# A four-layer attention/Fourier kernel: weight rows spread over more buffers, sequence products moved among TensorE's instructions

## The chip, the cores and the metric

One core of a Trainium2 chip runs the whole program in one launch. The metric is the device time of one execution in microseconds (us). Each kernel is run several times and the median is compared. The profile is one further execution on the same core, recorded by the hardware profiler. Engines are called PE (TensorE), PEld (its weight loads), DVE (VectorE), ACT (ScalarE), POOL (GpSimd) and SP (SyncE, which here issues nearly all DMAs).

## The reference

The input x has 2048 rows of 640 numbers in f32. Four layers follow one another, each added to its input:

```
x = x + A(layernorm(x));  x = x + B(layernorm(x));  x = x + A(layernorm(x));  x = x + B(layernorm(x))

A: qkv = x @ wqkv                     # 32 heads of 20
   row s looks at rows s, s-2, ..., s-14   # 8 keys, dilation 2, masked below 0
   o = softmax(q.k * 20**-0.5) . v
   return o @ wo
B: a = x @ dft_hid_re.T;  b = x @ dft_hid_im.T
   return dft_seq_re @ a - dft_seq_im @ b   # 2048 x 2048 sequence matrices
```

The matrices of B are inputs like any other: the kernel may not use that they hold sines and cosines.

## The kernel before

Every f32 matrix product is made of three fp32r products: each operand is split into a rounded high part (a cast, on ACT) and the remaining low part (a subtraction, on DVE or POOL), and high x high, high x low and low x high are added up in PSUM (`PASSES`). `split(hi, lo, src)` does this (L130 the cast, L132 and L134 the subtraction).

**Attention layers (`layer_a`, run for layers 0 and 2).** The 2048 rows are 4 chunks c of 4 tiles j of 128 rows. The loop is a plan written out by hand: `at(step, phase, fn, ...)` puts a piece of work into a step (about -8 to 66) and a phase, and the loop over steps and `PHASES` issues the pieces in that order on all engines (`manual_schedule(engines=ENGINES)`). Within a step the phases run `peT0 dma evac hi pe peL pe2 ... actL ... misc dmac dmar pe3w pe3`. One step holds half a unit of attention: the products q*k on DVE (L435) with a halving on POOL (L438) and a reduction on DVE (L445), the softmax on small tiles (L453 the exponential on ACT, L462 to L470 on DVE), the products with v on DVE (L475), and their sums on POOL (L494 to L496; the very last on DVE, L491). TensorE meanwhile makes qkv (`qkv_mm`, L366), transposes the attention output (`pc_pe`, L331; `pc_hi` casts it on ACT, L335; `pc_sub` subtracts the high part in PSUM with the negative identity, L339; `pc_lo` copies out the low part, L354, or on DVE, L352) and multiplies it by wo (`wo_mm`, L519). `wo_add` (L163, DVE) adds the residual out of PSUM and sums up for the layernorm; `wo_stats` (ACT L168, L170, L174), `wo_fin` (POOL L178), `ln_hi` or `ln_tail` (ACT L908, L924; DVE L925) and `ln_lo` (L912) make the split, normalized rows of the next layer.

**Sequence products in the attention layers.** The first of the eight output tiles of the following layer B is begun inside the attention layer. `z_mm(s, p)` (L979) adds the products of sequence tile s (16 of them) to five PSUM banks; p is a third of them, 5 matmuls of 128 x 512, and None is all 15. `ZTHIRDS[ly]` says how many thirds stand at which step; thirds at step 52 go into phase `pe2`, the others into `pe3`. The split sequence tile comes from DRAM (`c_get`, L957) or is loaded and split in place (`c_load` L934, `c_hi` L938, `c_lo` L966). Buffers s0, s2 and s3 take turns. After the last step the remaining pieces are issued in a written order: the transposes `pc_pe(67)`, `wo_mm` for tiles 2 and 3 of the last chunk, and `z_mm` for tiles 13, 14 and 15 with the layernorm tails between them.

**Spectral layers (`LayerB`).** `run` copies the first output tile out of PSUM (`evac`, `zt_put`, L1034 to L1041), calls `load_w`, and then goes on with the next tile's sequence products (`zpart`), of which only TensorE's order is written out. The order on the other engines, and the place of their DMAs on SP, is made by a scheduler when the program is built, also against the end of the attention layer. `load_w` loads the five row blocks of the two hidden matrices, real and imaginary in turn, ten loads of 320 KB through the two buffers of tag xa, and splits each (the imaginary ones negated) into r2a (real, after wo is done with it) and pr0 to pr3 and zo3 (imaginary; pr0 to pr3 are the product buffers of the attention layer). `ymm` (L1061) uses them. Meanwhile `x_whole` and `x_combine` (L1106 to L1120) make sums of row blocks and store them to DRAM through tags stg and xa for a Strassen-like scheme (`pair`, `product` L1158), which covers the other output tiles.

The tag stg has two buffers, used by `qkv_evac`, by `c_load`, and later by `x_combine`.

Of the kernel before, what the change touches and what calls it, by code (L numbers as in the profile page):

```python
# [11 lines left out]
F32R = mybir.dt.float32r  # L12
# [8 lines left out]
D = 640  # L21
# [5 lines left out]
P = 128  # L27
# [3 lines left out]
KD = D // P  # L31
# [15 lines left out]
WSTEP = (0, 0, 0, 1, 1, 2, 2, 3, 3, 4, 4, 5, 5, 6, 7)  # L47
WHOLE = ((43, 45, 47, 49, 51, 55, 57, 59, 63), (51, 57, 63))
ZTHIRDS = (
    {49: 3, 50: 3, 51: 2, 52: 1, 53: 2, 54: 1, 56: 3, 57: 6, 58: 3, 59: 4, 60: 2, 61: 1, 62: 3, 63: 4, 64: 1},  # L50
    {50: 3, 51: 5, 52: 1, 53: 1, 54: 1, 55: 1, 56: 5, 57: 4, 58: 3, 59: 3, 60: 1, 61: 1, 62: 4, 63: 2, 64: 4},
)
TA = 65
# [25 lines left out]
def tile_layers(ctx: ExitStack, tc: tile.TileContext, x, wqkv, wo, cs, wre, wim, out):  # L79
    nc = tc.nc  # L80
# [9 lines left out]
    def nm(base):  # L90
        uid[0] += 1
        return f"{base}_{uid[0]}"

    def T(shape, tag, dt=F32, bufs=1, pool=None):
        return (pool or sb).tile(shape, dt, tag=tag, name=nm(tag), bufs=bufs)

    def pt(shape, tag, bufs=1):
        return ps.tile(shape, F32, tag=tag, name=nm(tag), bufs=bufs)
# [30 lines left out]
    def split(hi, lo, src, neg=False, eng=None):  # L129
        nc.scalar.activation(hi, src, AF.Copy, scale=-1.0 if neg else 1.0)  # L130
        if neg:
            nc.vector.scalar_tensor_tensor(lo, src, -1.0, hi.bitcast(F32), op0=ALU.mult, op1=ALU.subtract)  # L132
        else:
            (eng or nc.vector).tensor_tensor(lo, src, hi.bitcast(F32), op=ALU.subtract)  # L134
# [62 lines left out]
    def load_x(src, j, tag="xa"):  # L197
        xt = T([P, D], tag, bufs={"xa": 2}.get(tag, 1))
        nc.sync.dma_start(xt, src[:, j, :])
        return xt  # L200
# [45 lines left out]
    def layer_a(li, stats, handoff, prev):  # L246
        xin, xout = xs[li], xs[li + 1]
        first = li == 0
# [19 lines left out]
        def at(step, phase, fn, *args):  # L268
            plan.setdefault((step, phase), []).append((fn, args))
# [41 lines left out]
        def pc_pe(step):  # L311
            banks, out = {}, []
            for kind, c, j, k0, k1, bank, col, tag in pieces[step]:
                if tag and tag.startswith("r1"):
                    if j == 2:
                        oT["pair"] = T([P, 2, 2, KD, P], tag, F32R)
                    oT[(c, j)] = oT["pair"][:, j - 2]
                elif tag:
                    (xnT if kind == "x" else oT)[(c, j, 1) if kind == "x" else (c, j)] = T([P, 2, KD, P], tag, F32R)
                src, st = (  # L320
                    (xnT[(c, j)], xnT[(c, j, 1)]) if kind == "x" else (oo[(c, j // 2)][:, j % 2], oT[(c, j)])
                )
                if bank not in banks:
                    banks[bank] = (pt([P, 512], bank), [])
                pb, todo = banks[bank]
                todo += [(pb[:, col + i * P : col + (i + 1) * P], src[:, k * P : (k + 1) * P]) for i, k in enumerate(range(k0, k1))]
                out.append((pb[:, col : col + (k1 - k0) * P], st, k0, k1))
            pieces[step] = out
            for pb, todo in banks.values():
                for i, (dst, src) in enumerate(todo):  # L330
                    nc.tensor.matmul(dst, src, ident, start=i == 0, stop=i == len(todo) - 1, is_transpose=True)  # L331

        def pc_hi(step):
            for pb, st, k0, k1 in pieces[step]:
                nc.scalar.copy(st[:, 0, k0:k1], pb.rearrange("p (k f) -> p k f", f=P))  # L335
# [12 lines left out]
        def pc_lo(step, vec=False):  # L348
            for pb, st, k0, k1 in pieces[step]:
                pv = pb.rearrange("p (k f) -> p k f", f=P)  # L350
                if vec:
                    nc.vector.tensor_tensor(st[:, 1, k0:k1], pv, st[:, 0, k0:k1].bitcast(F32), op=ALU.subtract)  # L352
                else:
                    nc.scalar.copy(st[:, 1, k0:k1], pv)  # L354
# [155 lines left out]
        def wo_mm(c, j, banks, e0=0, e1=2, k0=0, k1=KD):  # L510
            if e0 == 0 and k0 == 0:
                oT[(c, j, "m")] = []
            for e in range(e0, e1):
                if k0 == 0:
                    oT[(c, j, "m")].append(pt([P, 512], banks[e]))
                m = oT[(c, j, "m")][e]
                for i, (a, b) in enumerate(PASSES):
                    for k in range(k0, k1):
                        nc.tensor.matmul(  # L519
                            m[:, :320],  # L520
                            oT[(c, j)][:, a, k],
                            wo_s["w"][:, b, k, e * 320 : (e + 1) * 320],
                            start=(i, k) == (0, 0),
                            stop=(i, k) == (2, KD - 1),
                        )

        def wo_add(c, j, e0=0, e1=2, store=True):
            for e in range(e0, e1):
                if e == 0 and j == 0:
                    nstats[c] = Stats()  # L530
                nstats[c].add(j, e, xr[(c, j)], oT[(c, j, "m")][e][:, :320])
            if e1 == 2 and store:
                wo_store(c, j)
# [4 lines left out]
        def wo_stats(c, j):  # L538
            nstats[c].added(j, xr[(c, j)])

        def wo_fin(c, j0, j1):
            nstats[c].finish(j0, j1)
# [282 lines left out]
        thirds = [t for t, n in ZTHIRDS[ly].items() for _ in range(n)]  # L825
# [6 lines left out]
        for z in range(len(thirds) // 3):  # L832
            t = thirds[3 * z]
            if first and z in PRE:
                at((46, 47, 49)[z] if z < 3 else max(thirds[3 * z - 7] + 1, t - 3), "dmac", handoff.c_get, z)
            elif first:
                at(t - 2, "dmac", handoff.c_load, z)
                at(t - 1, "hi", handoff.c_hi, z)
                at(t - 1, "misc", handoff.c_lo, z, z in (11, 12))
            else:  # L840
                at(min(t - 1, 48 + z) if z < 3 else t - 1, "dmac", handoff.c_get, z)
            for p in range(3):
                at(thirds[3 * z + p], "pe2" if thirds[3 * z + p] == 52 else "pe3", handoff.z_mm, z, p)
        if first:
            at(62, "dmac", handoff.c_load, 13)
            at(63, "hi", handoff.c_hi, 13)
# [8 lines left out]
        with tc.manual_schedule(engines=ENGINES):  # L855
            if first:
                prologue_first()
            nc.vector.tensor_copy(mk, mask)
            for s in range(LEAD0[0], last + 1):
                for ph in PHASES:  # L860
                    for fn, args in plan.pop((s, ph), ()):
                        fn(*args)
            pc_pe(67)
            pc_hi(67)
            pc_lo(67, True)
            wo_mm(c, 2, None, 0, 2, 3)
            wo_mm(c, 3, ("pq", "aux0"))
            wo_add(c, 2)
            wo_stats(c, 2)
            wo_fin(c, 2, 3)  # L870
            if first:
                handoff.c_hl(14)
            handoff.z_mm(13, None)
            handoff.ln_tail(c, 2, xr, nstats)
            wo_add(c, 3)
            handoff.ln_lo(c, 2)
            handoff.z_mm(14, None)
            wo_stats(c, 3)
            wo_fin(c, 3, 4)
            if first:  # L880
                handoff.c_hl(15)
            handoff.ln_tail(c, 3, xr, nstats)
            handoff.ln_lo(c, 3)
            handoff.z_mm(15, None)
# [4 lines left out]
    class LayerB:  # L889
# [95 lines left out]
                )  # L985

        def load_w(self):
            self.wr = T([P, 2, KD, D], "r2a", F32R)
            self.wi = []
            for k in range(KD):  # L990
                raw = load_x(wre, k)
                split(self.wr[:, 0, k], self.wr[:, 1, k], raw)
                raw = load_x(wim, k)
                if k < 4:
                    wt = T([P, 2, D], f"pr{k}", F32R)
                    hl = (wt[:, 0], wt[:, 1])
                else:
                    wt = T([P, 2, D], "zo3", F32R)
                    hl = (wt[:, 0], wt[:, 1])
                split(hl[0], hl[1], raw, neg=True)  # L1000
                self.wi.append(hl)

        def cw_load(self, t, s):
            self.raw[s] = wtile([P, 512])
# [324 lines left out]
    st0 = [None] * NC  # L1329
    b1, b2 = LayerB(1), LayerB(3)  # L1330
    layer_a(0, st0, b1, None)
    st2 = [None] * NC
    b1.run(st2)
    layer_a(2, st2, b2, b1)
    b2.run(None)
    b2.ytile(NT - 1, 0, None)
# [56 lines left out]
```

## Time and profile before

| | us |
|---|---|
| three runs | 1764.7, 1770.85, 1773.08 |
| median | 1770.85 |
| profiled execution, its own time | 1764.77 |
| its span | 1762.9 |
| PE busy | 1735.4 (98%) |
| DVE busy | 1378.4 (78%) |
| ACT busy | 809.2 (46%) |
| POOL busy | 622.0 (35%) |

The span runs from the first to the last recorded instruction; the execution's own time has some us around it. Matmuls are pipelined, and the busy time of PE counts each until its modelled end, so a busy PE is not one at its peak. In the rows of a timeline stand the start, the duration, the engine, the line of the kernel, the operation, the tiles (output <- inputs) and, in brackets, how long the engine had been idle before and what ended that. "x30" merges 30 instructions of a kind. A line of the waits says who waited for whom: us in total, times, longest. In the span the first attention layer ends near 390 us, the second runs from about 860 to 1262 us.

### The profile page before, as it was taken

What the parts mean: (1) busy time and instruction counts of PE and PEld (TensorE: products, weight loads), DVE (VectorE), ACT (ScalarE), POOL (GpSimd) and SP (SyncE); (2) the same over time, 40 slices, a digit from 0 to 9 for tenths busy, and PEclk for the clock granted to TensorE, in tenths of its full rate; (3) what the DMA queues carried; (4) which work ended last, traced back from release to release, by engine and by line L of the source; (5) the groups of instructions that cost most, each with busy time, mean ns of one, the idle gap of its engine ahead of it and who ended that gap; (6) DMA issues with size and microseconds to landing.
All of it is one profiled execution on the core that took longest, in us unless ns stands there. A gap on an engine that the chain in (4) does not pass through costs nothing.

```text
span 1762.9 us, 26454 instructions
## 1 busy us (share of the span) xinstructions
PE 1735.4 (98%) x8798; PEld 1506.6 (85%) x8798; DVE 1378.4 (78%) x2131; ACT 809.2 (46%) x1682; POOL 622.0 (35%) x585
## 2 busy tenths in 40 slices
PE   9999998989999999999999999999999999999999
PEld 7889897878888888888998889988788888888888
DVE  6999999988767767767648999999777676687673
ACT  4564544554445444445534344444434443443441
POOL 4799998840000000000028998899100000000000
PEclk9999999999999999999999999999999999999999
DMA  8996769748777777686657866798587767767761
GB/s 287 314 317 206 224 205 327 263 166 309 266 254 252 247 252 229 223 272 224 201 182 228 270 209 214 218 332 275 196 311 261 253 212 246 253 217 244 253 202 53
DMA packets 273961, 426.20 MB, mean 242 GB/s; under 512 B 22656, under 2 KB 153728, under 8 KB 273568
## 3 DMA queue, kind: packets, MB, share of 16 engines
q1 hardware_dynamic: 270624, 422.54, 72.2%
q10 hardware_dynamic: 3200, 1.97, 0.4%
q8 instruction: 70, 1.15, 0.3%
q14 instruction: 67, 0.55, 0.1%
HBM read 339.28 MB, written 85.14 MB: 241 GB/s over the span
## 4 chain that ended last, share of the span: by engine, by line
PE 69%; DVE 15%; DMA 7%; POOL 3%; issue 3%; ACT 3%; SPq 0%; DVEq 0%; ACTq 0%; POOLq 0%
PE m L366 14%; PE aux L1061 14%; PE t L1158 11%; PE m L1158 11%; PE pq L1158 5%; PE xt L1158 5%; PE aux L519 4%; DVE pr L435 3%; DVE pr L475 2%; DMA xc<-stg 2%; DVE lg L445 1%; POOL pr L494 1%; PE m L979 1%; PE t L979 1%; DMA xa<-wre_in 1%
## 5 line engine op out<-in xcount | busy, mean ns | idle before, releaser
L366 PE MATMUL m<-r,s 128*128 128x480 f32 x1920 | 436.1, 381 | 0.4 <-DVE r L649 0.2
L366 PEld LDWEIGHTS m<-r,s 128*128 128x128 f32 x1920 | 355.6, 188 | 53.8 <-DVE r L649 1.0
L1061 PE MATMUL aux<-r2a,zo 128*128 128x320 f32 x768 | 226.5, 310 | 0.0
L1151 ACT CAST r<-win 128x512 fp32r<-128x512 f32 x246 | 150.2, 620 | 159.7 <-DVE win L1187 65.4
L494 POOL TENSOR_TENSOR pr<-pr 128x640 f32<-128x640 f32 x126 | 206.3, 1637 | 32.3 <-DVE pr L475 31.5
L1061 PE MATMUL aux<-pr,zo 128*128 128x320 f32 x704 | 208.3, 308 | 0.0
L178 POOL TENSOR_TENSOR stats<-stats,mhalf 128x1 f32<-128x1 f32 (+1 forms) x40 | 29.4, 734 | 497.0 <-ACT stats L174 487.7
L1152 DVE TENSOR_TENSOR r<-win,r 128x512 fp32r<-128x512 f32 x246 | 165.5, 687 | 46.4 <-ACT r L1151 44.4
L435 DVE TENSOR_TENSOR pr<-pq,win 128x1280 f32<-128x1280 f32 x128 | 189.7, 1483 | 8.9 <-ACT pq L408 5.8
L475 DVE TENSOR_TENSOR pr<-pq,win 128x1280 f32<-128x1280 f32 x128 | 190.7, 1491 | 5.0
L438 POOL TENSOR_TENSOR pr<-pr 128x640 f32<-128x640 f32 x116 | 166.8, 1438 | 15.6 <-DVE pr L435 15.2
L1158 PE MATMUL m<-r,r 128*128 128x512 f32 x594 | 152.6, 392 | 0.0
L1061 PEld LDWEIGHTS aux<-r2a,zo 128*128 128x128 f32 x768 | 144.1, 188 | 1.9
L1158 PE MATMUL t<-r,r 128*128 128x512 f32 x498 | 135.7, 394 | 0.0
L1061 PEld LDWEIGHTS aux<-pr,zo 128*128 128x128 f32 x704 | 132.2, 188 | 2.1
L1158 PEld LDWEIGHTS m<-r,r 128*128 128x128 f32 x594 | 111.4, 188 | 24.6
L979 PE MATMUL m<-s,r 128*128 128x512 f32 x384 | 118.6, 396 | 4.9 <-POOL s L966 1.7
L445 DVE TENSOR_REDUCE lg<-pr 128x64 f32<-128x640 f32 (+1 forms) x128 | 112.1, 876 | 8.9 <-POOL pr L438 8.5
L979 PE MATMUL t<-s,r 128*128 128x512 f32 x384 | 118.2, 395 | 0.4 <-DVE ot L1036 0.3
L495 POOL TENSOR_TENSOR pr<-pr 128x320 f32<-128x320 f32 x126 | 112.1, 890 | 9.9
L1158 PEld LDWEIGHTS t<-r,r 128*128 128x128 f32 x498 | 93.9, 188 | 21.6
L373 ACT COPY stg<-m 128x480 f32<-128x480 f32 x128 | 71.0, 555 | 84.9 <-PE m L366 64.3
(295 smaller groups left out, 3216.1 us busy)
## 6 DMA issues: line engine op xcount, KB each, us to landing
win<-cs_in SPq DMA_DIRECT2D x351, 256.0 KB, 3.8
r<-xc SPq DMA_DIRECT2D x240, 256.0 KB, 4.2
win<-kvb SPq DMA_DIRECT2D x96, 440.0 KB, 4.3
xa<-cs_in SPq DMA_DIRECT2D x121, 256.0 KB, 4.1
win<-kvb SPq DMA_DIRECT2D x64, 360.0 KB, 4.9
kvb<-stg SPq DMA_DIRECT2D x60, 320.0 KB, 5.2
xc<-stg SPq DMA_DIRECT2D x32, 512.0 KB, 4.0
s<-c0b SPq DMA_DIRECT2D x26, 512.0 KB, 5.8
```

What stands on the lines that cost most here:

```text
L366: nc.tensor.matmul(mt[g][:, : 3 * F], st[:, a, k], wq[q][:, b, k], start=n == 0, stop=n == 14)
L435: nc.vector.tensor_tensor(pr, q, wview(u, jp, 0, [[1, FE]]), op=ALU.mult)
L438: nc.gpsimd.tensor_tensor(pv[:, :, 0:10], pv[:, :, 0:10], pv[:, :, 10:20], op=ALU.add)
L445: nc.vector.tensor_reduce(lgs[u][:, :, 2 * jp : 2 * jp + 2].rearrange("p h j w -> p (j w) h"), prq.pop((u, jp)), axis=AX.X, op=ALU.add,)
L475: nc.vector.tensor_tensor(pr.rearrange("p j w (h d) -> p j w h d", d=DH), lgs[u][:, :, 2 * jp : 2 * jp + 2].rearrange("p h j w -> p j w h" ...
L494: g.tensor_tensor(pr[:, :, 0:4], pr[:, :, 0:4], pr[:, :, 4:8], op=ALU.add)
L495: g.tensor_tensor(pr[:, :, 0:2], pr[:, :, 0:2], pr[:, :, 2:4], op=ALU.add)
L979: self.last = nc.tensor.matmul(self.z[t][k], self.xn[c][:, a, j, k * P : (k + 1) * P], self.ct[s][:, b], start=s == 0 and i == 0, stop=s = ...
L1061: self.last = nc.tensor.matmul(self.ym[e][:, :320], zt[(k, a, ri)][:, j2 * P : (j2 + 1) * P], w[:, e * 320 : (e + 1) * 320], start=(k, a, ...
L1151: nc.scalar.copy(hi, raw)
L1152: nc.vector.tensor_tensor(lo, raw, hi.bitcast(F32), op=ALU.subtract)
L1158: nc.tensor.matmul(bank, w(a, kb), hl[b], start=start and (a, b) == (0, 0), stop=stop and (a, b) == (1, 0),)
```

## The change

Three things are changed. (1) In the first attention layer four thirds of sequence products stand at step 52, none at 53 and 54 (before: one, two and one), and in this layer those of step 52 go into phase `pe`, ahead of the products of `pc_sub`, where they stood behind them. (2) In the second attention layer two thirds of tile 13 are issued ahead of the last transposes, and the third at the place where all three stood. (3) `load_w` issues its loads into tiles of its own: the first real and the first imaginary row into the two stg buffers, the second ones into the two xa buffers, and the rest through xa; and r2a is taken over only after the first load has been issued.

```diff
 ZTHIRDS = (
-    {49: 3, 50: 3, 51: 2, 52: 1, 53: 2, 54: 1, 56: 3, 57: 6, 58: 3, 59: 4, 60: 2, 61: 1, 62: 3, 63: 4, 64: 1},
+    {49: 3, 50: 3, 51: 2, 52: 4, 56: 3, 57: 6, 58: 3, 59: 4, 60: 2, 61: 1, 62: 3, 63: 4, 64: 1},
...
-                at(thirds[3 * z + p], "pe2" if thirds[3 * z + p] == 52 else "pe3", handoff.z_mm, z, p)
+                at(thirds[3 * z + p], "pe" if first and thirds[3 * z + p] == 52 else "pe2" if thirds[3 * z + p] == 52 else "pe3", handoff.z_mm, z, p)
...
+            for p in range(0 if first else 2):
+                handoff.z_mm(13, p)
             pc_pe(67)
...
-            handoff.z_mm(13, None)
+            for p in range(0 if first else 2, 3):
+                handoff.z_mm(13, p)
...
         def load_w(self):
-            self.wr = T([P, 2, KD, D], "r2a", F32R)
-            self.wi = []
-            for k in range(KD):
-                raw = load_x(wre, k)
-                split(self.wr[:, 0, k], self.wr[:, 1, k], raw)
-                raw = load_x(wim, k)
-                if k < 4:
-                    wt = T([P, 2, D], f"pr{k}", F32R)
-                    hl = (wt[:, 0], wt[:, 1])
+            self.wr = None
+            self.wi = [None] * KD
+            tags = ("stg", "stg", "xa", "xa")
+            for n, (x, k) in enumerate([(x, k) for k in range(KD) for x in "ri"]):
+                raw = T([P, D], tags[n] if n < 4 else "xa", bufs=2)
+                nc.sync.dma_start(raw, (wim if x == "i" else wre)[:, k, :])
+                if x == "i":
+                    wt = T([P, 2, D], f"pr{k}" if k < 4 else "zo3", F32R)
+                    self.wi[k] = wt[:, 0], wt[:, 1]
+                    split(wt[:, 0], wt[:, 1], raw, neg=True)
                 else:
-                    wt = T([P, 2, D], "zo3", F32R)
-                    hl = (wt[:, 0], wt[:, 1])
-                split(hl[0], hl[1], raw, neg=True)
-                self.wi.append(hl)
+                    if self.wr is None:
+                        self.wr = T([P, 2, KD, D], "r2a", F32R)
+                    split(self.wr[:, 0, k], self.wr[:, 1, k], raw)
```

## The prediction

> **What bounds the kernel now.** I read the page first, then the list of who waited for whom on TensorE, then the table of stretches, and last the timelines of the two attention tails.
>
> ```profile
> span 1762.9 us, 26454 instructions
> PE 1735.4 (98%) x8798; PEld 1506.6 (85%) x8798; DVE 1378.4 (78%) x2131; ACT 809.2 (46%) x1682; POOL 622.0 (35%) x585
> PE 69%; DVE 15%; DMA 7%; POOL 3%; issue 3%; ACT 3%; SPq 0%; DVEq 0%; ACTq 0%; POOLq 0%
> ```
>
> TensorE (PE) is busy 1735.4 of 1762.9 us: all of its idle time is 27.5 us, so no edit that only fills waits can take more than that, plus what a slowed clock costs. The profiled execution took 1764.77 us, 1.9 more than its span, and is the lowest but for 0.07 us of the three times (1764.7, 1770.85, 1773.08). I make the sum against 1764.77 and take the same difference off the median, 1770.85. Half a per cent, 8.85 us, is about what a measurement of this kernel can tell from no change.
>
> ```profile
> PE aux L339 <- ACT s L335: 5.6, 4, 3.8
> PE pq L331 <- POOL zo L496: 2.5, 2, 1.9
> ```
>
> ```profile
> 291.60:298.30 6.70, 5.37 (x16) 4.42 (x17) 6.44 (x10) 4.67 (x15) 6.39 (x8) 0.50 1.01 375
> 284.00:372.00 88.00, 78.80 (x404) 67.84 (x402) 83.19 (x116) 40.55 (x99) 78.29 (x73) 0.94 0.74 253
> 1236.20:1243.80 7.60, 4.84 (x26) 3.70 (x27) 6.09 (x7) 1.68 (x5) 4.22 (x5) 1.00 0.32 115
> 1243.90:1247.20 3.30, 3.30 (x14) 3.22 (x13) 1.51 (x6) 0.00 (x0) 0.00 (x0) 0.50 0.00 0
> ```
>
> The two longest waits in the list lie where the change puts products: 3.8 us in the first attention layer, 1.9 us in the second. (In the table the columns are stretch, length, busy time of PE, PEld, DVE, ACT, POOL, granted clock, DMA share, GB/s.) Behind each wait follows a stretch at clock 0.50: 6.7 us, of which PE was busy 5.37, and 3.3 us, all busy. So a filled wait may be worth its length and half of the busy time behind it. The second row is the reservation: from 284 to 372 us, the second half of the first layer, DVE is busy 83.19 of 88 us, PE only 78.80. There DVE sets the pace, and time saved on PE counts only where DVE waits for PE.
>
> **First layer: three more thirds at step 52 (z_mm, 5 products each).**
>
> ```profile
> 283.85 0.63 PE L979 MATMUL m<-s,r 128*128 128x512 f32 x2
> ...
> 285.01 0.62 PE L979 MATMUL m<-s,r 128*128 128x512 f32 x2
> ...
> 292.93 0.58 PE L339 MATMUL aux<-ot,nident 128*128 128x256 f32 x1 [3.81 <-ACT s L335]
> 296.30 5.60 PE L519 MATMUL aux<-r2a,ot 128*128 128x320 f32 x30
> 301.73 4.56 PE L519 MATMUL aux<-r2a,s 128*128 128x320 f32 x30
> ```
>
> ```profile
> 295.40 0.31 ACT L453 ACTIVATE lg<-lg 128x128 f32<-128x128 f32 x1 [1.97 <-DVE lg L464]
> 295.61 0.36 ACT L354 CAST ot<-aux 128x256 fp32r<-128x256 f32 x1
> 301.93 0.49 DVE L163 SCALAR_TENSOR_TENSOR r<-aux,r 128x320 f32<-128x320 f32 x1 [1.56 <-PE aux L519]
> 313.06 0.49 DVE L163 SCALAR_TENSOR_TENSOR r<-aux,r 128x320 f32<-128x320 f32 x1 [0.68 <-PE aux L519]
> ```
>
> One third takes 285.01 - 283.85 = 1.16 us. The wait begins at 292.93 - 3.81 = 289.12; after it, four thirds (one was there, behind the subtracting products of L339; three come from steps 53 and 54) fill 4 x 1.16 = 4.64 us, to 293.76. The four products of L339 take at most 4 x 0.58 = 2.3 us, so PE is done by 296.1 and stands again: the output products (L519) need the low parts from ACT's L354, which ran at 295.61 behind the exponential of 295.40, and that waited for DVE. Nothing in this chain comes earlier, so L519 starts at 296.30 as before. The gain is the clock: 30 products at full speed take about 4.5 us (the second row of L519) where they took 301.73 - 296.30 = 5.43, so DVE's wait of 1.56 shrinks by about 1.0. Without fillers between the next output tiles PE delivers earlier still, and the 0.68 us wait goes too. PE then waits for DVE's additions, which costs nothing, as DVE sets the pace. So DVE comes to the layer's end earlier by 1.7 us if the clock stays full, and by 0.2 if the slow stretch only moves (then the 1.56 grows by some 0.5 and 0.68 goes). Both are as likely, since PE now stands near 295; I take **-1.0** us (0 to -2.2). The load of the seventh sequence tile from c0b moves up one step on SP, past one qs and one window load; its buffer is free by then, since its third was moved up. Cost 0.
>
> **Weights (load_w).** Ten rows of 320 KB in the order r0, i0, r1, i1, ... The first two now go to stg, not xa. The order of the built program shows three moves.
>
> ```profile
> 360.18 0.38 SPq L199 DMA_DIRECT2D xa<-x_in  x1
> ...
> 365.89 0.33 SPq L199 DMA_DIRECT2D xa<-wre_in  x1
> ...
> 369.71 2.37 DVE L491 TENSOR_REDUCE zo<-pr 128x160 f32<-128x1280 f32 x1
> ...
> 372.72 0.65 ACT L335 CAST zo<-pq 128x256 fp32r<-128x256 f32 x2 [5.09 <-PE pq L331]
> ...
> 373.40 0.76 DVE L352 TENSOR_TENSOR zo<-pq,zo 128x256 fp32r<-128x256 f32 x2 [1.32 <-ACT zo L335]
> ```
>
> ```profile
> 1145.10 0.53 SPq L383 DMA_DIRECT2D qb<-stg  x1
> 1148.96 0.33 SPq L536 DMA_DIRECT2D xs<-xr  x1
> ...
> 1160.53 1.21 SPq L421 DMA_DIRECT2D win<-kvb  x2
> 1163.51 0.58 SPq L400 DMA_DIRECT2D qs<-qb  x1
> ```
>
> The loads: in the first layer both issue in SP's empty 360.6 to 365.9; in the second between 1145.6 and 1148.96 and between 1161.7 and 1163.51, where SP waits for other engines. Queued behind each are a store or a qs load that start later anyway: 0.
>
> The splits: the cast and the subtraction of i0 now stand on ACT and DVE ahead of the last transposes' cast (L335) and subtraction (L352). i0 goes to buffer pr0, which the last reduction (L491) reads until 369.71 + 2.37 = 372.08. The same kinds of operation take 0.74 on ACT and 0.82 on DVE (L130 at 1256.62 and L132 at 1257.40, below). So ACT is free at 372.9 instead of waiting at 372.72, and DVE turns to L352 at 373.7 instead of 373.40. TensorE's last output products wait for both: **+0.3** us in each layer (0.1 to 0.8). In return the casts of r0 and r1 stand ready where xa rows were waited for, and the evacuations of the sequence sums have fewer subtractions ahead: in the first layer I give that -0.2.
>
> **Second layer: two of three thirds of tile 13 ahead of the last transposes.**
>
> ```profile
> 1241.86 0.33 PE L331 MATMUL pq<-ident,zo 128*128 128x128 f32 x1 [1.90 <-POOL zo L496]
> 1242.40 0.55 PE L331 MATMUL pq<-ident,zo 128*128 128x128 f32 x3 [0.21 <-DVE zo L491]
> 1243.40 3.23 PE L519 MATMUL aux<-r2a,zo 128*128 128x320 f32 x12 [0.46 <-ACT zo L335]
> ...
> 1251.23 0.62 PE L979 MATMUL m<-s,r 128*128 128x512 f32 x2
> ...
> 1258.13 1.52 PE L979 MATMUL m<-s,r 128*128 128x512 f32 x6
> ...
> 1263.38 0.94 PE L979 MATMUL m<-s,r 128*128 128x512 f32 x3 [0.98 <-DVE zo L1041]
> ```
>
> ```profile
> 1251.43 0.74 ACT L130 ACTIVATE r2a<-xa 128x640 fp32r<-128x640 f32 x1 [0.83 <-PE aux L519]
> 1256.62 0.74 ACT L130 ACTIVATE pr<-xa 128x640 fp32r<-128x640 f32 x1 [1.16 <-DMA xa<-wim_in]
> ```
>
> ```profile
> 1255.49 0.83 DVE L912 TENSOR_TENSOR r<-win,r 128x640 fp32r<-128x640 f32 x1 [0.67 <-ACT r L924]
> 1257.40 0.82 DVE L132 SCALAR_TENSOR_TENSOR pr<-xa,pr 128x640 fp32r<-128x640 f32 x1 [1.08 <-ACT pr L130]
> ```
>
> Ten products, 2 x 1.16 = 2.32 us, start at 1241.86 - 1.90 = 1239.96 and end at 1242.28, before the last transposes could run (1242.40). They leave the stretch from 1251.23 on: **-2.3**. With the gap filled the 3.3 us at half clock should go: **-1.6**. Late next is tile 15, the last: its low part came from L912 at 1255.49 + 0.83 = 1256.3, 1.8 us ahead of its start at 1258.13. PE arrives 3.6 us earlier; that chain moves too, as it starts from the output products, but only by the 1.6 of the clock and less 0.74, since a second cast (r1) now stands on ACT at 1251.43 ahead of its statistics. So its low part is there at about 1255.5 and PE, at 1254.5 to 1254.9 (the first two products need only the high part), waits some 0.5: **+0.5** (0 to 1.5). The 0.98 us wait for an evacuation (L1041) shrinks by half at most, as i1 still is ahead of it: **-0.3**. With the +0.3 above this layer gives -3.4 (-1.5 to -4.8).
>
> Later stages keep what is gained: from 500 to 864 us and at the end PE sets the pace.
>
> **The sum.** First layer -1.0 + 0.3 - 0.2 = -0.9; second -3.4; together **-4.3 us**, 1764.77 to 1760.5 in the profile, 1770.85 to **1766.5** in the median (0.24%, within what counts as the same).
>
> **The rivals.**
> 1. *PE's lead counts in full.* For: the chain that ended last is 69% PE. Against: DVE's 83.19 of 88 us. Then the first layer gives 3.81 + 5.37/2 = 6.5 us and the second 2.3 + 1.6 + 1.0 = 4.9 less 0.3: together -11.1, 1759.7, faster by 0.63%. Chance 0.28.
> 2. *The slow stretch stays or moves* to the critical products of a tail. The row: behind a wait of 1.9 us in the second layer the clock fell to 0.50 for 3.3 us. If it is not this gap that brings it, only the gap itself is won: -4.3 + 1.6 + 1.0 = -1.7, 1769.1. Chance 0.12. (The Trainium skill, "TensorE: Matmul & The Clock Gate", section "HAM oscillation", asks only that idle gaps stay below about 3.4 us; by that rule a gap of 1.9 us would cost no clock. The trace speaks against it, unless several gaps in one window add up.)
> 3. *Slower: the sequence casts queue behind weight rows.* On ACT and DVE the splits of i1 to i4 stand, in order, among those of the sequence tiles (L938) of the next stage; PE has only two split tiles in hand, 7 us.
>
> ```profile
> 1258.85 1.85 SPq L1005 DMA_DIRECT2D win<-cs_in  x2
> 1262.59 0.33 SPq L199 DMA_DIRECT2D xa<-wre_in  x1
> ```
>
> ```profile
> 1265.82 0.74 ACT L130 ACTIVATE r2a<-xa 128x640 fp32r<-128x640 f32 x1 [1.49 <-DMA xa<-wre_in]
> ```
>
>  A row issued at 1262.59 was cast at 1265.82, 3.2 us later; with cast and subtraction that is 4.8 us a round in two buffers, 2.4 us a row, faster than the 3.5 us that PE takes for a tile. It decides if SP holds the rows back by a window load, as between 1258.85 and 1262.59: then a round takes 8.5 us, 4.3 a row, 0.8 more than PE's pace, for six or seven rows in each layer: some +10 for the two, less what is won early, -1: 1779.9, slower by 0.5%. Against: the rows start one round earlier than before and PE had no such wait. Chance 0.08.
>
> **How the numbers follow.** Forecast 0.52, rivals 0.28, 0.12, 0.08. Faster by over 0.5%: 0.28, and 0.02 of the forecast's own upper end; slower 0.08; the same 0.62. The likeliest case alone spans 1763.5 to 1769. The range takes in rivals 1 and 2 and the spread of the three times: 1759 to 1773.
>
> **What would show it.** Right: no clock of 0.50 near 1244; the transposes of 1241.86 without idle before them; L519 near 296 with a wait of 1 to 2 us ahead of it; DVE's wait of 1.56 at 0.5; the first layer's L491 earlier by 1 us. Wrong: L491 earlier by 4 us or more (rival 1), a 0.50 stretch over the products behind 373 or 1243 (rival 2), sequence products waiting for their casts on ACT or DVE right behind a weight row's (rival 3).

## The result, and the profile after

The changed kernel took 1761.26 us (median of six, 1758.93 to 1762.41) against 1768.76 for the kernel before (six, 1764.7 to 1773.08): a ratio of 0.9958, 95% interval 0.9942 to 0.9973, or 7.5 us less by the medians. Measured again beside later experiments it was 0.9977 (0.9964 to 0.9990), 1764.12 us against 1767.85, 3.7 less. The forecast was 4.3 us less, to 1766.5 in the range 1759 to 1773. The sign was right (both intervals lie below 1), and half a per cent is not passed; the size fits the second measurement and is 3 us too small for the first.

The profiled execution of after took 1758.93 us, 5.8 less than the one of before. Its page, the same three lines:

```profile
span 1757.1 us, 26454 instructions
PE 1731.3 (99%) x8798; PEld 1501.6 (85%) x8798; DVE 1375.7 (78%) x2131; ACT 807.6 (46%) x1682; POOL 621.2 (35%) x585
PE 83%; DVE 7%; DMA 4%; POOL 3%; issue 2%; ACT 1%; SPq 0%; DVEq 0%; ACTq 0%; POOLq 0%
```

The instructions are the same 8798 on PE. Its busy time fell by 1735.4 - 1731.3 = 4.1 us, its idle time from 27.5 to 25.8, by 1.7. So in the balance most of the 5.8 us is clock: waits were filled, but new ones came. The list of who waited for whom on PE:

```profile
PE m L982 <- DMA s<-c0b: 4.9, 3, 2.3
PE pq L331 <- POOL zo L496: 1.9, 1, 1.9
PE aux L339 <- ACT s L335: 1.8, 3, 0.7
```

The wait of 3.8 us (L339 for L335) is gone, and one of the two on POOL in front of the last transposes; the other, in the first layer, is still there. At the top now stand waits for sequence tiles from c0b, 0.7 us in all before: one of 1.00 at 291 (the load that the prediction moved up at cost 0; it is hidden, as L519 still waits for ACT behind it), and two near 1153 and 1163, behind SP's wait that is shown below. The stretches of the prediction, and one more, at 370.7 (columns as there):

```profile
291.60:298.30 6.70, 5.95 (x34) 5.09 (x33) 6.40 (x11) 4.67 (x15) 6.39 (x8) 1.00 1.02 364
284.00:372.00 88.00, 77.19 (x411) 65.89 (x410) 83.88 (x119) 41.73 (x102) 77.95 (x73) 0.99 0.76 261
370.70:374.10 3.40, 3.36 (x12) 3.36 (x13) 1.75 (x5) 0.26 (x1) 0.00 (x0) 0.50 0.00 0
1236.20:1243.80 7.60, 6.91 (x40) 5.66 (x39) 6.44 (x7) 1.27 (x3) 2.99 (x3) 1.00 0.13 42
1243.90:1247.20 3.30, 3.30 (x25) 3.30 (x24) 0.74 (x5) 1.54 (x6) 0.55 (x1) 1.00 0.26 99
```

Both stretches at 0.50 of the forecast now run at 1.00. One of 3.4 us is left in the whole span (its last half us aside), at 370.7, on the first layer's last output products. The profiled execution of before had four: the two of the prediction, one at 366.7 and one at 708.0.

**First layer, TensorE and then VectorE of after.**

```profile
291.10 0.73 PE L982 MATMUL m<-s,r 128*128 128x512 f32 x2 [1.00 <-DMA s<-c0b]
...
294.71 0.28 PE L339 MATMUL aux<-ot,nident 128*128 128x256 f32 x1
...
296.09 4.66 PE L519 MATMUL aux<-r2a,ot 128*128 128x320 f32 x30 [0.75 <-ACT s L354]
300.60 4.56 PE L519 MATMUL aux<-r2a,s 128*128 128x320 f32 x30
305.94 4.66 PE L519 MATMUL aux<-r2a,r 128*128 128x320 f32 x30 [0.78 <-DVE r L163]
...
369.60 0.66 PE L331 MATMUL pq<-ident,zo 128*128 128x128 f32 x4 [1.92 <-POOL zo L496]
370.74 3.55 PE L519 MATMUL aux<-r2a,zo 128*128 128x320 f32 x12 [0.48 <-ACT zo L335]
```

```profile
300.79 0.49 DVE L163 SCALAR_TENSOR_TENSOR r<-aux,r 128x320 f32<-128x320 f32 x1 [0.68 <-PE aux L519]
...
367.35 2.31 DVE L491 TENSOR_REDUCE zo<-pr 128x160 f32<-128x1280 f32 x1
```

L339 follows the thirds without idle, L519 starts at 296.09 (before 296.30) behind a wait of 0.75 us, and its first 30 products take 4.51 us to the next group instead of 5.43. DVE's wait of 1.56 is 0.68, PE now waits for DVE's additions (0.78), and the last reduction starts at 367.35, 2.36 us earlier. Of this, 1.2 are lost again in the tail: its first 12 products take 3.55 us at half clock, where those of before took 2.17 at full clock (the stretch had passed at 370.1).

**Second layer, the tail on TensorE of after.**

```profile
1235.76 2.65 PE L519 MATMUL aux<-r2a,zo 128*128 128x320 f32 x17
1238.25 0.62 PE L982 MATMUL m<-s,r 128*128 128x512 f32 x2
...
1240.57 0.94 PE L331 MATMUL pq<-ident,zo 128*128 128x128 f32 x4
1241.99 2.37 PE L519 MATMUL aux<-r2a,zo 128*128 128x320 f32 x12 [0.48 <-ACT zo L335]
...
1248.60 0.62 PE L982 MATMUL m<-s,r 128*128 128x512 f32 x2
...
1253.50 2.06 PE L982 MATMUL m<-s,r 128*128 128x512 f32 x6 [0.18 <-ACT r L927]
...
1258.79 0.93 PE L982 MATMUL m<-s,r 128*128 128x512 f32 x3 [0.40 <-ACT zo L1037]
```

The transposes follow the two thirds without idle, and the products take 2.37 us where they took 3.23. PE is done with the products ahead of the gap at 1235.76 + 2.65 = 1238.41, before at 1239.96: 1.55 us earlier. At the tail's end it is 4.59 earlier (1258.79 against 1263.38). So the tail gave 3.0 us.

Between the layers something went the other way. On SP and DVE of after:

```profile
1140.06 0.38 SPq L382 DMA_DIRECT2D kvb<-stg  x1
1140.49 0.53 SPq L383 DMA_DIRECT2D qb<-stg  x1
1145.64 0.34 SPq L996 DMA_DIRECT2D stg<-wre_in  x1
1146.08 0.38 SPq L536 DMA_DIRECT2D xs<-xr  x1
...
1147.77 0.93 SPq L421 DMA_DIRECT2D win<-kvb  x2
```

```profile
1155.31 1.49 DVE L435 TENSOR_TENSOR pr<-pq,win 128x1280 f32<-128x1280 f32 x1 [1.62 <-DMA win<-kvb]
...
1166.52 1.49 DVE L435 TENSOR_TENSOR pr<-pq,win 128x1280 f32<-128x1280 f32 x1 [1.69 <-DMA win<-kvb]
```

The weight row goes into the staging buffer whose two stores stand right ahead of it on SP. SP waits 4.6 us for them (1141.02 to 1145.64), and with it the windows for DVE, which waits 1.62 and 1.69 us. Most of the 4.6 us SP would have stood anyway: the next store (xs<-xr) is issued 5.6 us after the one of qb here, and 3.9 us after it in before (1148.96 against 1145.10), so 1.7 us are new. By the starts of the same multiplications in both traces DVE is 4.8 us ahead of before at 1140 us and 1.6 ahead at 1170.

And 3.2 of the 5.8 us are no part of the change. They come near 704 us, in a spectral layer that the change does not touch. VectorE in before and in after, and the stretch behind it in before:

```profile
703.62 0.69 DVE L1187 TENSOR_TENSOR win<-xa,win 128x512 f32<-128x512 f32 x1 [4.48 <-issue]
```

```profile
700.61 0.69 DVE L1190 TENSOR_TENSOR win<-xa,win 128x512 f32<-128x512 f32 x1 [3.24 <-DMA win<-cs_in]
```

```profile
708.00:711.40 3.40, 3.40 (x10) 2.65 (x9) 3.15 (x6) 2.15 (x4) 0.00 (x0) 0.50 0.97 341
```

This instruction waits in the trace of every kernel here, 2.8 to 4.5 us. Seven of the fourteen traces name a window load from cs_in as what ended the wait; the others, before among them, name nothing. In before PE waited behind it and fell to half clock. So it did in e5 and e11, and in no other trace. From 690 to 720 us after's lead on PE grows from 1.4 to 4.6 us. So the two profiles balance as: first layer -1.2, this place -3.2, small differences on the way to 1140 us -0.4, SP's wait +3.2, second tail -3.0, after 1300 us -1.2; together -5.8. The last are two waits of PE in before, 0.23 us at 1308 and 0.94 at 1316, for the low part of a sequence tile (L966, on DVE). After has none there; why is not shown.

### The profile page after: what moved, and what is told of

It is laid out like the page before. It is cut to its first block, busy times and chain, and to the rows that moved or that the text cites. A ratio compares the mean times of both kernels' runs of the same rounds, so it can differ in the third digit from the quotient of the medians.

```text
span 1757.1 us, 26454 instructions
## 1 busy us (share of the span) xinstructions
PE 1731.3 (99%) x8798; PEld 1501.6 (85%) x8798; DVE 1375.7 (78%) x2131; ACT 807.6 (46%) x1682; POOL 621.2 (35%) x585
## 4 chain that ended last, share of the span: by engine, by line
PE 83%; DVE 7%; DMA 4%; POOL 3%; issue 2%; ACT 1%; SPq 0%; DVEq 0%; ACTq 0%; POOLq 0%
PE m L366 20%; PE aux L1064 16%; PE t L1161 11%; PE m L1161 11%; PE pq L1161 6%; PE xt L1161 6%; PE aux L519 4%; PE t L982 3%; PE m L982 3%; DVE pr L475 2%; DMA win<-kvb 2%; PE xt L982 2%; DVE pr L435 1%; DVE lg L445 1%; POOL pr L494 1%
```

## The experiments

Each row is a kernel's ratio to the one before, measured on one chip with it. The ratio is the recorded one; the quotient of two medians can differ from it by 0.15% (e2: 1768.07 against 1768.12 on its chip). "Clock" is the mean granted clock over all executions of that kernel; 0.001 of it is 2 x 0.001 x 1763 = 3.5 us at half clock.

| kernel | ratio (95%) | median us | clock |
|---|---|---|---|
| before (84 executions) | 1 | 1768.4 | 0.9948 |
| after, first | 0.9958 (0.9942 to 0.9973) | 1761.26 | 0.9987 |
| after, again | 0.9977 (0.9964 to 0.9990) | 1764.12 | 0.9981 |
| e1, thirds of step 52 alone | 0.9985 (0.9970 to 1.0001) | 1766.51 | 0.9974 |
| e2, tile 13 alone | 0.9985 (0.9971 to 1.0000) | 1768.07 | 0.9955 |
| e3, weights alone | 0.9990 (0.9973 to 1.0007) | 1766.65 | 0.9952 |
| e4, e1 and e2 together | 0.9973 (0.9960 to 0.9986) | 1765.14 | 0.9974 |
| e5, stg only in the first spectral layer | 0.9976 (0.9964 to 0.9988) | 1763.21 | 0.9980 |
| e6, tile 13 in both layers | 0.9975 (0.9962 to 0.9988) | 1762.66 | 0.9990 |
| e7, e5 and e6 together | 0.9967 (0.9951 to 0.9982) | 1761.87 | 0.9987 |
| e10, stg loads later on SP | 0.9958 (0.9943 to 0.9973) | 1761.73 | 0.9990 |
| e11, e10 and e6 together | 0.9960 (0.9945 to 0.9975) | 1761.71 | 0.9991 |

**The clock over all executions.** The 84 executions of before alone spread from 1762.8 to 1775.8 us, and their time goes with their clock: four at 0.992 took 1773.4 on average, 34 at 0.995 1767.8, one at 0.998 1764.0. The fitted line is 1.85 us (standard error 0.17) for each 0.001, half of the 3.5 us at half clock. From before to after (0.9983 over both rows, 18 executions) the time at half clock falls from 18.4 to 6.1 us. By the line this is worth 6.5 us; the mean time fell from 1768.64 to 1762.88, 5.8. That is an agreement of sizes, not a proof that each us of it lay on the path; and the waits that bring slow stretches cost time of their own, which is in the line too.

**e1: the thirds of step 52 alone.** `ZTHIRDS` and the phase as after; tile 13 and `load_w` as before.

> Only the four thirds at step 52 of the first attention layer. Theory (DVE sets the pace there): the first layer's last reduction L491 starts 2.2 to 2.6 us earlier than in the kernel before, because DVE's waits of 1.56, 0.68 and 0.52 us go; what of it reaches the sequence products behind the tail depends on where the next half-clock stretch falls: total -1 to -2.5 us. Rival (PE's lead counts in full): -5 us or more in total. Rival (the gain of the whole change is not from here): 0, L491 where it was.

L491 starts at 368.05 us against 369.71, 2.2 earlier when the 0.5 us are counted by which this execution was already behind at step 52 (e2 and e3, without this edit: 0.3). The stretch of 6.8 us at half clock near 291 is in before, e2 and e3, and in no trace of the kernels with the edit. Over all executions the clock gains 0.0026, 9 us at half clock; the total, 0.9985, is not told from 1. In the second tail, unfilled here, the wait and its slow products stand:

```profile
1239.77 0.39 PE L331 MATMUL pq<-ident,zo 128*128 128x128 f32 x1 [1.91 <-POOL zo L496]
...
1241.67 3.57 PE L519 MATMUL aux<-r2a,zo 128*128 128x320 f32 x12 [0.46 <-ACT zo L335]
```

**e2: tile 13 alone.** Only `for p in range(0 if first else 2): handoff.z_mm(13, p)` and its rest are kept.

> Only the two thirds of tile 13 ahead of the last transposes of the second attention layer. Theory: the gap of 1.9 us (2.3 us of products) and the half-clock stretch behind it (1.6 us) both go: -3 to -4.5 us between the transposes and the first products of the next stage. Rival (the slow stretch is not brought by this gap): -2.3 us, and a 0.50 stretch still stands within 5 us behind it.

The tail gives 3.0 us, and the stretch near 1244 is gone. The total does not show it: 0.9985. Some of it is lost at 1284 us (e4 shows how), and the first layer's stretch fell on the tail's products at 372.9, as in after.

**e3: the weights alone.** Only the new `load_w`.

> Only the weight rows' change. Theory: in the second attention layer the first weight load stands on SP behind the stores of its own staging buffer and holds the queue some 4.5 us; the window loads behind it come late and DVE loses about 3 us there (two waits of 1.6 us on win<-kvb, as in the whole change); the tails gain under 0.7 us: +2 to +3 us in total. Rival (the loads are hidden, the tails gain): -0.5 to -2 us, no wait of DVE on win<-kvb over 1 us.

A loss was expected, and there is none that shows: 0.9990. The DVE waits came (1.9 us in two), and 2.5 us were won in the second tail. 1.2 of them are the slow stretch that before had there: the wait of 1.90 us ahead of the last transposes is in e3 too, but no slow stretch follows it (the last section shows how that can be).

**e4: both product edits, weights as before.**

> Both moves of sequence products, weights as before. Theory: the sum of the first two single edits, -5 to -7 us, and faster than the whole change by some 2 to 3 us, since the whole change loses that much to the weight loads in the second attention layer. Rival (the weights' part helps): slower than the whole change, -3 to -5 us.

The expected lead over the whole change did not come: without the edit of the weights, which had cost 3.2 us in the profile of after, the ratio is 0.9973, against 0.9958 and 0.9977 with it. The cast of the last imaginary row (i4, to zo3) on ACT, in before, e4 and after:

```profile
1281.05 0.74 ACT L130 ACTIVATE zo<-xa 128x640 fp32r<-128x640 f32 x1 [0.79 <-DMA xa<-wim_in]
```

```profile
1283.21 0.74 ACT L130 ACTIVATE zo<-xa 128x640 fp32r<-128x640 f32 x1 [4.92 <-DMA xa<-wim_in]
```

```profile
1273.74 0.74 ACT L130 ACTIVATE zo<-xa 128x640 fp32r<-128x640 f32 x1 [0.44 <-DMA xa<-wim_in]
```

And what it does to TensorE in e4, with the stretch behind it:

```profile
1284.00 0.42 PE L1064 MATMUL aux<-zo,ot 128*128 128x320 f32 x1 [2.99 <-ACT zo L130]
```

```profile
1286.00:1289.40 3.40, 3.40 (x11) 2.84 (x10) 3.13 (x7) 1.14 (x2) 0.00 (x0) 0.50 0.94 339
```

PE arrives some 3.5 us earlier and meets a row that came just in time before. The wait of 2.99 us and the half clock give back 5 us. With four rows loaded early (after) the last one is cast 7.3 us sooner than in before, and PE, 4.6 us ahead there, does not wait for it. So in these traces the weights' edit, which shows no gain alone, is what keeps the tail's gain; how often it does is not shown, since e5 and e7 have the late row in their profiles and mean clocks near after's.

**after, again.** The changed kernel once more beside the next kernels.

> The whole change once more, beside the next three kernels. All theories: 0.993 to 0.998 of the kernel before. DVE's two waits on win<-kvb near 1150 to 1170 us come again if the weight loads bring them, and may be absent if they are a chance of that one execution; the first layer's L491 starts 1.9 to 2.4 us earlier than in the kernel before either way.

DVE's waits for windows came again, smaller (1.5 us in two), and PE lost nothing by them here: its lead over before is 2.6 us at 1150 and 2.8 at 1180. An evacuation wait that the prediction had hoped to shrink was longer:

```profile
1258.41 1.19 PE L982 MATMUL m<-s,r 128*128 128x512 f32 x3 [2.10 <-DVE zo L1039]
```

Behind it follow 3.4 us at half clock (from 1259.0), and PE's lead falls from 5.4 to 2.8 us. In e6 a wait of 1.92 us at the same place does the same, from 4.2 to 1.4.

**e5: no staging buffers in the second spectral layer.**

```diff
-            tags = ("stg", "stg", "xa", "xa")
+            tags = ("stg" if self.li == 1 else "xa",) * 2 + ("xa", "xa")
```

> The whole change, but the second spectral layer loads all its weight rows through xa, so that no weight load stands on SP inside the second attention layer. Theory (the load behind its staging buffer's stores holds SP): no wait of DVE on win<-kvb over 1 us between 1140 and 1175 us, and 1 to 3 us faster than the whole change. Rival (window loads come late there anyway, from DMA traffic): the waits are as in the whole change and the time is the same within 1 us, or 1 us slower, since the tail loses the early rows.

The waits on windows are gone, and the last row is late as in e4 (e5's timeline):

```profile
1286.26 0.64 PE L1064 MATMUL aux<-zo,ot 128*128 128x320 f32 x1 [2.88 <-ACT zo L130]
```

Half clock follows for 6.8 us in that execution. The cause was right, the sum wrong: 0.9976, where the whole change beside it has 0.9977.

**e6 and e7: tile 13 ahead in both layers.** `range(2)` in place of `range(0 if first else 2)`; e7 has e5's line too.

> The whole change, and the two thirds of tile 13 ahead of the last transposes in the first attention layer too. Theory: the gap of 1.9 us before those transposes and the half-clock stretch over the output products behind it go: 2 to 4 us faster than the whole change. Rival (the layernorm tail of the last tiles becomes the end of the chain): under 1 us, with a new wait of PE ahead of tile 15.

> Both of the two edits before on top of the whole change. Theory: the sum, 3 to 7 us faster than the whole change. Rival (each only moves a wait): no faster than the better of the two.

The first layer's wait of 1.9 us is gone, and no slow stretch lies on the products (e6, its timeline and its stretch):

```profile
370.78 2.29 PE L519 MATMUL aux<-r2a,zo 128*128 128x320 f32 x12 [0.46 <-ACT zo L335]
```

```profile
369.00:372.30 3.30, 2.83 (x16) 2.12 (x15) 2.17 (x5) 1.35 (x3) 0.45 (x1) 1.00 0.00 0
```

This place gains 2.7 us over after up to 380 us. 1.5 of them are left at 400, behind a wait of 1.10 us for an evacuation at 388. The total does not resolve it: 0.9975, beside 0.9977 for the whole change. e7 shows e4's late row again (its PE waits 2.48 us there, and 6.8 us at half clock follow); at 0.9967 it cannot be told from e6 or after.

**e10 and e11: the stg loads later on SP.** The loads into stg are issued behind the load of qs of unit 30, at 1198 us instead of 1146 and 1161; e11 has e6's edit too.

```diff
-                nc.sync.dma_start(raw, ...)
+                with tc.issue_after(self.mark[30].ins):
+                    nc.sync.dma_start(raw, ...)
```

> The whole change, with one thing moved: in the second attention layer the two weight loads into staging buffers are issued some 45 places later on SP, behind the last but one qs load, long after the staging buffers' last stores. Theory (the load stands behind its own buffer's stores and holds the queue, and early rows are needed where the next stage's last weight row is due): no wait of DVE on win<-kvb over 1 us between 1140 and 1175, no wait of PE on the last row's cast near 1284; 1.5 to 3 us faster than the whole change in the stage table. Rival (the waits on window loads are DMA traffic): as the whole change, waits on win<-kvb of 1.5 us or more.

> The same, and the two thirds of tile 13 ahead of the last transposes in the first attention layer too. Theory: another 1.5 to 2 us at the first layer's tail (no gap before the last transposes, no half-clock stretch behind it): 0.993 to 0.996 of the kernel before, the fastest of all. Rival (each only moves a wait): 0.996 to 0.998, as the whole change.

```profile
1198.24 0.42 SPq L998 DMA_DIRECT2D stg<-wre_in  x1
1198.71 0.42 SPq L998 DMA_DIRECT2D stg<-wim_in  x1
```

DVE's waits for windows from 1130 to 1180 us in before, after, e1 and e10 (us in total, times, longest):

```profile
DVE pr L435 <- DMA win<-kvb: 0.3, 1, 0.3
```

```profile
DVE pr L435 <- DMA win<-kvb: 3.3, 2, 1.7
```

```profile
DVE pr L435 <- DMA win<-kvb: 3.0, 1, 3.0
```

```profile
DVE pr L435 <- DMA win<-kvb: 0.7, 1, 0.7
```

Every kernel that loads into stg at the early place has these waits: two in after, its second execution, e3, e6 and e12 below, one in e13 below, 1.5 to 3.4 us in total. Those without (e2, e4, e5, e7, e10, e11) have none or one of at most 1.0, but for e1: with the old weights it had one of 3.0, so late windows have another cause as well. Nor does PE wait for a row near 1284 in e10 and e11. Both signs are as expected. The gain over the whole change is not shown: the totals, 0.9958 and 0.9960, equal after's better measurement, and the intervals overlap with its other one.

**e12: one third of tile 13 ahead, not two**, to see how much of the gap must be filled. One execution.

> The whole change with one third (5 products, 1.16 us) instead of two ahead of the second attention layer's last transposes. If a gap of some 1 us in a window brings half clock, a 0.50 stretch stands between 1240 and 1250 us; if it takes more, none does, and PE only waits 0.8 to 1.1 us.

```profile
1249.93 0.33 PE L331 MATMUL pq<-ident,zo 128*128 128x128 f32 x1 [0.76 <-POOL zo L496]
```

A wait of 0.76 us is left, another of 0.23 follows, and there is no half clock from 1240 to 1255. Its 1771.15 us hold two DVE waits for windows and four slow stretches elsewhere, and say nothing of the edit. Nor does this one trace show that a third is enough, since e3 had no half clock there with the whole wait.

**e13: 30 products fewer** in the first layer's second half, 7 us of PE's work. One execution.

> The whole change with the 30 products of sequence tiles 5 and 6 left out in the first attention layer (7 us of PE's work after step 56; the output is not the reference's). Theory (DVE sets the pace from 284 to 372 us): L491 and the last transposes of that layer come within 0.5 us of where they are in the whole change, PE idles 7 us more. Rival (PE's lead counts in full): they come 5 to 7 us earlier.

```profile
284.00:372.00 88.00, 73.52 (x382) 62.81 (x380) 83.80 (x119) 41.67 (x102) 79.09 (x74) 0.96 0.78 265
```

```profile
368.52 2.38 DVE L491 TENSOR_REDUCE zo<-pr 128x160 f32<-128x1280 f32 x1
```

PE is busy 73.52 us instead of after's 77.19, DVE 83.80 instead of 83.88, and L491 starts at 368.52 against 367.35: 1.2 us later, which is what this execution was behind already at 292 us. The work left out turned into a PE wait of 4.2 us. DVE sets the pace there.

## Why the prediction was right, and where not

- **What bounds the kernel**: right. DVE paces the first layer's second half; e13 shows it. Rival 1 falls with it: 7 us less on PE bring L491 nothing, and in after it came 2.4 us earlier, not 4 or more. The first measurement, 1761.26, lies nearer to rival 1's 1759.7 than to 1766.5, but that has other causes (below).
- **The chain at step 52**: right in each link (296.09, the wait of 0.75, 4.51 us for 30 products, PE then waiting for DVE). Taken was -1.0 between 0 and -2.2; L491 moved by -2.2 in e1, the end where the clock stays full. That I weighed both ends alike was wrong: no trace with the edit had the stretch. The "wait of 1 to 2 us" ahead of L519 was 0.75, and DVE's 1.56 became 0.68, not 0.5.
- **The first layer's tail**: forecast +0.3 - 0.2; measured +1.2 in after. Not the splits did it (the wait for the cast L335 is 0.48 us, before 0.46), but rival 2's event: the slow stretch on the critical products. It is there in after, its second execution, e2, e3, e4 and e5. In before, e1, e10 and e13 it came ahead of the last transposes instead, where DVE hides most of it (their wait shrinks to 0.4 to 0.6 us); e12 had both. With the gap filled (e6, e7, e11) there was none. So the layer as a whole gave -1.2 where -0.9 was forecast, out of terms that were both mis-sized.
- **SP's loads at no cost**: the step that failed. "Queued behind each are a store or a qs load that start later anyway" took the staging buffer to be long free. Its stores stand right ahead, SP waits 4.6 us for them, 1.7 longer than it stood in before, and window loads stand behind it: 1.5 to 3.4 us of DVE waits, 3.2 us in the profile of after. e10 moves the loads, and the waits go, but for one of 0.7.
- **The second layer's tail**: -3.4 forecast, -3.0 measured in after and e2. The gap, its slow stretch and the +0.5 at tile 15 (x6 in 2.06 us instead of 1.52) came as worked out. The evacuation wait (0.98 before) was 0.40 in after, 2.10 in the second execution of it and 1.92 in e6, the last two with half clock behind them, 2.6 to 2.7 us in all. So "shrinks by half" is not shown, and where this wait is long it takes back most of the tail's gain; what sets its length stays open.
- **What is late next**: tile 15 was named, the last weight row at 1284 us was not. The prediction gave the weights' edit -0.2 of readiness in the first layer; e4, e5 and e7 show that in the second the tail's gain hangs on it. Rival 3 had the mechanism (rows held on SP between window loads, cast late), but in the changed kernel the early rows prevent it. The wait stands in e2, e4, e5 and e7, which load no rows early there.
- **The size**: that 4.3 lies near the 3.7 of the second measurement and the 5.8 of the profiles is in part luck: SP's wait (+3.2 in the profile) was not in the sum, and 3.2 of the profiles' difference are no part of the change. The clock terms were -1.0 and -1.6, for 10 us at half clock. Over all executions 12.3 us of half clock went, which by before's own spread goes with 6.5 us. A single profile of before could not show that: it had 0.995, as the average has, but which stretches are critical changes from one execution to the next. What of the 3.7 to 7.5 us belongs to which edit, beyond the two tails, stays open: e1, e2 and e3 alone give 0.15, 0.15 and 0.10%, and each of these intervals reaches 1.

No version is shown to beat the whole change; e10 and e11 equal its better measurement.

## What to carry to other kernels

Before a filled wait is counted, look for the input that came just in time behind it: an edit that shows nothing alone (rows loaded early) can be what keeps another's gain. The load into a reused buffer held the queue here until the buffer's stores had ended, so read which instruction last used that very buffer, how long the queue would have stood anyway, and what stands behind the load. Where the clock falls after short waits, add up the idle time window by window (next section) and compare the mean clock over many executions; between two single profiles, 3 us can be chance.

## What the runs showed of the hardware

Stretches at half clock were 3.41 or 6.83 us long, and in each trace their starts lie whole multiples of 3.41 us apart: in before 291.56, 366.65, 707.98 and 1243.88 us, which is 22, 100 and 157 times. So a trace can be cut into windows of 3.41 us that fit its slow stretches, and the time without a matmul on PE can be added up in each window. Over the fourteen traces, for windows at full clock:

| idle time of PE in the window | windows | followed by half clock |
|---|---|---|
| under 1.2 us | 7080 | 0 |
| 1.2 to 1.9 us | 49 | 10 |
| 1.9 us and more | 19 | 19 |

So several short waits count together, and a wait that a boundary cuts counts in two parts. The last transposes of the second layer waited 1.90 us in before and in e3. In before the window behind 1240.46 held most of it and the small waits next to it: PE busy 1.34 of 3.41 us, 2.07 idle, and half clock followed. In e3 the wait was cut at 1248.17, 1.72 us were idle, and none followed:

```profile
1240.46:1243.87 3.41, 1.34 (x7) 0.92 (x8) 2.09 (x2) 0.65 (x2) 1.27 (x2) 1.00 0.00 0
```

```profile
1244.76:1248.17 3.41, 1.69 (x12) 1.42 (x10) 3.38 (x3) 0.00 (x0) 2.83 (x3) 1.00 0.21 74
```

The windows' place against the instructions moves from one execution to the next. In the first layer's tail, where the wait was unfilled, a slow stretch lay between 365 and 378 us in all eleven traces, but on critical products in some and on hidden ones in others. Where it came early (before, e1, e10, e12 and e13), the window ahead of it held 1.3 to 1.7 us of other, shorter waits. Near 289 us the three traces without the edit of step 52 had 2.3 to 2.9 us idle in a window, those with it at most 1.62. The two bounds of the table are read off these same traces, and what decides between them stays open. The Trainium skill ("TensorE: Matmul & The Clock Gate", section "HAM oscillation") asks that idle gaps stay below about 3.4 us; here a wait of 2.10 us, alone in its window, was followed by half clock (the second execution of after, at 1258.41).
